# Placing the rows of a Z block on every third partition, in three transfers

## The chip, the cores and the metric

The kernel runs on one core of one Trainium2 chip. The metric is the device time of one execution in microseconds (us). Most quantities below come from one execution that the hardware profiler recorded.

## What is computed

For a batch of 8 sequences of 5696 positions and 128 channels, the reference makes a long convolution by FFT and then a spectral mix:

```python
Xf = np.fft.rfft(x, n=2*S, axis=1)
Hf = np.fft.rfft(h, n=2*S, axis=0)
a = np.fft.irfft(Xf * Hf[None], n=2*S, axis=1)[:, :S, :]      # [8, 5696, 128]
X = np.fft.rfft(a, axis=1)                                      # its first 64 modes are used
Yr = einsum('bmd,mde->bme', Xr, w_r) - einsum('bmd,mde->bme', Xi, w_i)
Yi = einsum('bmd,mde->bme', Xr, w_i) + einsum('bmd,mde->bme', Xi, w_r)
u = a + np.fft.irfft(Y, n=S, axis=1)
out = u + maximum(u @ w_ch, 0)                                  # float32
```

## The kernel before

**The work.** The transform length 2S = 11392 is split as 89 x 128. The kernel does both parts as matrix products in f16: a product over the 45 rows of a sequence that hold data (`a_tile`, `h_tile` and the loop before it), and one over 128 with the matrices `m_sb`. Only 45 of the 89 frequencies of the first part are needed, so a spectrum has 90 rows, 45 real and 45 imaginary parts. The batch is taken as 4 pairs (`g_` from 0 to 3). For each pair, `tick` runs over 23 pairs of frequencies: products on TensorE into `Xs`, multiplication with the spectrum of h on VectorE, the way back over 128 on TensorE into `Zs` (the Z values), a transfer of `Zs` into the DRAM scratch `zscr`, and the products that sum up the 64 modes. After the fourth pair the modes are mixed with the weights `W`.

**The final stage.** `u_tile(i, b)` reads the Z values back in another order. The scratch is cut into 32 blocks, 8 to a pair of sequences. A block is 90 rows (the 45 complex frequencies) of 4096 f16 values, 8 KB a row and 64 KB apart in DRAM, 720 KB in all. `load_zt(i)` fetches block i into one of 15 places: 4 in the tile `Xin` (`x_sb`), 4 in `As`, 7 in `MH`. These tiles held the input, its first transform and the matrices before, so a block waits until its place is free (`after`). Blocks 0 to 3 are issued on GpSimd's queue while the last pair is computed, blocks 4 to 14 on SP when that pair ends, and block i+15 on SP once block i has been used. In `u_tile` a Z block is the stationary operand of 16 products with the matrix `fq_sb`, which carries out the last step of the inverse transform; one product with `ib_sb` adds the inverse of the mixed modes. `Z0` and `Z1` are the first partition of the block and the one behind its last: partitions 19 to 108. The products read partitions 0 to 108, and the matrix has zeros in rows 0 to 18. `o_tile` then multiplies by `w_ch`, applies the maximum on ScalarE (L615), adds on VectorE (L616) into one of 20 `O` tiles, and SP sends it out. An output tile is 256 KB, or 208 or 192 KB at the end of a sequence.

**Order.** A small recorder (`R.add`) lists the instructions of each engine in program order and works out the semaphore waits from named tokens: `reads` and `writes` for data, `after` for other instructions. Each engine issues in that order, so an instruction that waits holds up all behind it on that engine, transfers included. A transfer takes the next semaphore of its ring (`R.rings`); one that takes a semaphore again waits for the transfer that had it.

**The head.** SP issues a few constants, then a row of zeros for the unused half of the last row of each of the two sequences in `x_sb` (tokens `xz`), and then the six pieces of the matrices `m_sb` (tile `MH`), which wait for the first piece of h. After them it issues further constants and filters. GpSimd issues h in three pieces, and then x in six (`x_pieces(0)`), which wait for the second piece of h and for the fourth piece of the matrices. All transfers are recorded by one helper, so they have one line, L283; matrix products are L286, evacuations L276 to L280.

Of the kernel before, what the change touches and what calls it, by code (L numbers as in the profile page):

```python
# [4 lines left out]
P = 128  # L5
# [118 lines left out]
def bass_long_conv_fft__then__afno_spectral_mix_kernel(nc, x, h, moe_w_r, moe_w_i, moe_w_ch, out):  # L124
# [8 lines left out]
    NQ = (NA + 1) // 2  # L133
# [3 lines left out]
    NT = (NQ + 1) // 2  # L137
# [16 lines left out]
    back = 4096.0 / L * np.where(kk == 0, 1.0, 2.0)  # L154
    step = pow(P, -1, NA)
    NW = NA + NQ - 1
    ph = 2.0 * np.pi * ((np.outer(kk, P * np.arange(NW))) % NA) / NA
    fq = np.zeros((P, NW))
    Z0 = 64 - NQ
    Z1 = 64 + NQ  # L160
    fq[Z0:Z1:2] = back[:, None] * np.cos(ph)
    fq[Z0 + 1:Z1:2] = -back[:, None] * np.sin(ph)
    tt = np.arange(N)
    ang = 2.0 * np.pi * np.outer(tt, np.arange(M)) / S
    modes = np.concatenate([np.cos(ang), -np.sin(ang)], axis=1)
# [9 lines left out]
    def const(name, a):  # L175
        return nc.inline_tensor(np.ascontiguousarray(a.astype(np.float16)), name=name)
# [10 lines left out]
    c_z = const("cZ", np.zeros((1, 64 * D)))  # L187
    zs = nc.dram_tensor("zscr", [NP * 2 * NQ * P, 2 * D], F16, kind="Internal")
# [6 lines left out]
    def at(name, cols, dt, off):  # L195
        return nc.alloc_sbuf_tensor_at(name, [P, cols], dt, offset=off)
# [16 lines left out]
    x_sb = at("Xin", P * D, F16, a_x)  # L213
# [23 lines left out]
    NC = 15  # L237
    zt = [(x_sb, P * D, i * 4096) for i in range(4)] + [(a_sb, 2 * AW, i * 4096) for i in range(4)]
# [12 lines left out]
    def ap(t, row, p0, n, off, dims):  # L251
        return bass.AP(t, p0 * row + off, [[row, n]] + [list(d) for d in dims])
# [4 lines left out]
    def pv(bank, off, dims, p0=0, n=P):  # L257
        return bass.AP(ps, p0 * 4096 + bank * 512 + off, [[4096, n]] + [list(d) for d in dims])

    R = Recorder(nc)  # L260
# [3 lines left out]
    def bank(i):  # L264
        return ("bank", i)
# [3 lines left out]
    def evac(dst, src, reads, writes, scale=None, eng=None, after=()):  # L269
        e = eng  # L270
        if e is None:
            turn[0] ^= 1
            e = "scalar" if turn[0] else "vector"
        if e == "scalar":
            if scale is None:
                return R.add(e, lambda h_: h_.copy(dst, src), reads, writes, after=after)  # L276
            return R.add(e, lambda h_: h_.activation(dst, src, COPY, scale=scale), reads, writes, after=after)  # L277
        if scale is None:
            return R.add(e, lambda h_: h_.tensor_copy(dst, src), reads, writes, after=after)  # L279
        return R.add(e, lambda h_: h_.tensor_scalar_mul(dst, src, scale), reads, writes, after=after)  # L280

    def dma(eng, dst, src, ring, reads=(), writes=(), after=()):
        return R.add(eng, lambda h_: h_.dma_start(dst, src), reads, writes, ring=ring, after=after)  # L283

    def mm(o, l, r, st, sp, reads, writes):
        return R.add("tensor", lambda h_: h_.matmul(o, l, r, start=st, stop=sp), reads, writes)  # L286
# [3 lines left out]
    def tile2(slots=3):  # L290
        slot[0] = (slot[0] + 1) % slots
        return 2 * slot[0]
# [4 lines left out]
    half = 64 * D  # L297
    dma("sync", fh_sb[:, :], c_fh.ap(), "c", (), [("fh",)])
    dma("sync", h_in[64 + NQ - 1:64 + NQ, :], c_z.ap(), "c", (), [("hz",)])
    dma("sync", f1_sb[:, :], c_f1.ap(), "c", (), [("f1",)])  # L300
    for b in range(2):
        dma("sync", x_sb[(b + 1) * NQ - 1:(b + 1) * NQ, half:], c_z.ap(), "c", (), [("xz", b)])

    def x_pieces(g_):
        for b in range(2):
            p0, off = b * NQ, x.offset + (2 * g_ + b) * S * D
            for c in range(2):
                yield (x_sb[p0:p0 + NQ - 1, c * half:(c + 1) * half],
                       bass.AP(x.tensor, off + c * half, [[P * D, NQ - 1], [1, half]]), ("xin", b, c))
            yield (x_sb[p0 + NQ - 1:p0 + NQ, 0:TAIL * D],  # L310
                   bass.AP(x.tensor, off + (NQ - 1) * P * D, [[TAIL * D, 1], [1, TAIL * D]]), ("xin", b, 2))

    h_loads = [dma("gpsimd", h_in[64 * c:64 * c + NQ - 1, :],
                   bass.AP(h.tensor, h.offset + c * half, [[P * D, NQ - 1], [1, half]]), "x", (), [("hin", c)])
               for c in range(2)]
# [5 lines left out]
    m_loads = []  # L321
# [2 lines left out]
            m_loads.append(dma("sync", m_sb[i][:, c * CH:(c + 1) * CH], bass.AP(c_m, i * KW + c * CH, [[2 * KW, P], [1, CH]]), "c",  # L324
                (), [("m", i, c)], after=h_loads[:1]))
    for dst, src, tok in x_pieces(0):
        dma("gpsimd", dst, src, "x", (), [tok], after=[h_loads[1], m_loads[3]])
    dma("sync", wi_sb[:, P:2 * P], c_i.ap(), "c", (), [("i16",)])
    dma("sync", fq_sb[:, :], c_fq.ap(), "c", (), [("fq",)])
    dma("sync", wv_sb[:, :], c_w.ap(), "c", (), [("wv",)])  # L330
# [20 lines left out]
    for j in range(16):  # L351
        t = tile2(4)
# [142 lines left out]
    def done_with(toks):  # L495
        return [r for tok in toks for r in R.readers.get(tok, [])[-2:]]

    def load_zt(i):
        g_, c = divmod(i, 8)
        j = i % NC  # L500
        after = []
        if i < 4:
            after = done_with(XT_[:6])
        elif i < NC:
            after = done_with(AST[:1])
            if i >= 8:
                after += done_with([("m", r, c_) for r in range(3) for c_ in range(NCH)] + HST)
        t, row, o = zt[j]
        dma("gpsimd" if i < 4 else "sync", ap(t, row, Z0, 2 * NQ, o, [[1, 4096]]),
            bass.AP(zs, g_ * 2 * NQ * P * 256 + c * 4096, [[P * 256, 2 * NQ], [1, 4096]]),  # L510
            "t" if i < 4 else "u", [("zd", g_, s) for s in range(NT)], [("zt", j)], after=after)

    X_AT = (1, 4, 7, 10, 13, 14)
    W_AT = (16, 18, 20)
# [2 lines left out]
    for g_ in range(NP):  # L517
        more = list(x_pieces(g_ + 1)) if g_ + 1 < NP else []
        todo_a = list(range(32)) if more else []
        for t in range(NT + LM):  # L520
            done = tick(g_, t)
            if t in X_AT and more:
                dst, src, tok = more.pop(0)
                dma("gpsimd", dst, src, "x", (), [tok], after=[done])
            if t in W_AT:
                load_w([done])
            if g_ == NP - 1 and t == NT:
                dma("sync", ib_sb[:, :], c_ib.ap(), "c", (), [("ib",)], after=done_with(AST[:1]))
            if g_ == NP - 1:
                for _ in range(ZT_AT.get(t, 0)):  # L530
                    load_zt(zt_next)
                    zt_next += 1
            if t >= NT:
                for _ in range(4):
                    if todo_a:
                        a_tile(todo_a.pop(0), False)
        modes_out(g_)
        while todo_a:
            a_tile(todo_a.pop(0), True)
        modes_turn(g_)  # L540
# [18 lines left out]
    for b in range(B):  # L559
        bk = 2 + b // 4  # L560
        for half_, yy in ((0, yr), (1, yi)):
            o = ps16[64 * half_:64 * half_ + 64, bk * 1024 + (b % 4) * P:bk * 1024 + (b % 4) * P + P]
# [13 lines left out]
    def u_tile(i, b):  # L576
        g_, c = divmod(i, 8)
        t = tile2(4)
        zt_, row, zo = zt[i % NC]
        for hb in range(2):  # L580
            o = pv(t + hb, 0, [[1, 360]])
            mm(o, c_sb[:, (2 * g_ + b) * P:(2 * g_ + b + 1) * P],
               ib_sb[:, (c * 16 + hb * 8) * NQ:(c * 16 + hb * 8 + 8) * NQ], True, False,
               [("c", g_ // 2), ("ib",)], [bank(t + hb)])
            for pl in range(8):
                o2 = (hb * 8 + pl) * 256 + b * P
                f0 = step * (c * 16 + hb * 8 + pl) % NA
                mm(pv(t + hb, pl * NQ, [[1, NQ]]), ap(zt_, row, 0, Z1, zo + o2, [[1, P]]), fq_sb[0:Z1, f0:f0 + NQ],
                   False, pl == 7, [("zt", i % NC), ("fq",)], [bank(t + hb)])
        ub = i // 2 % 2 * 2 + b  # L590
        n_ev[0] += 1
        evac(bass.AP(u_sb[ub], i % 2 * 16, [[UW, P], [32, NQ], [8, 2], [1, 8]]),
             pv(t, 0, [[1, NQ], [512, 2], [NQ, 8]]), [bank(t), bank(t + 1)],
             [("u", ub, i % 2)], after=g_done, eng="scalar" if n_ev[0] % 8 in (0, 2, 3, 5, 7) else "vector")
# [28 lines left out]
    for v in range(4 * NP):  # L623
        order = [(i, b) for i in (2 * v, 2 * v + 1) for b in range(2)]
        for n, (i, b) in enumerate(order):
            u_tile(i, b)
            for _ in range((2, 1, 2, 1)[n]):
                if todo:
                    o_tile(*todo.pop(0))
            if b and i + NC < 8 * NP:  # L630
                load_zt(i + NC)
        todo = [(v, b, qg) for b in range(2) for qg in range(3)]
# [34 lines left out]
```

## Time and profile before

| What | us |
|---|---|
| median of 3 runs (lowest, highest) | 474.1 (472.33, 479.89) |
| the profiled execution | 469.47 |
| its span, the basis of the profile's times | 467.6 |
| TensorE busy, share of the span | 405.6, 87% |
| VectorE, ScalarE busy | 332.7 and 331.1, 71% each |
| GpSimd busy | 27.6, 6% |
| SP's and ScalarE's hardware queue, share of 16 DMA engines | 57.6% |
| GpSimd's software queue, share of 16 DMA engines | 28.7% |

Times in the profile count from the start of the span. A line such as `45.09 16.84 PE ps L286 x128` of the chain means: at 45.09 us, for 16.84 us, 128 products of L286 on TensorE (PE). SPq and POOLq are the instruction queues of SP and GpSimd; PEld is the load of a stationary operand. The chain is followed back from the last instruction, at each step to what released it. A transfer appears under destination and source: `MH<-cM` are the matrices, `Xin<-zscr`, `As<-zscr` and `MH<-zscr` Z blocks, `out_dram<-O` outputs.

### The profile page before, as it was taken

What the parts mean: (1) busy time and instruction counts of PE and PEld (TensorE: products, weight loads), DVE (VectorE), ACT (ScalarE), POOL (GpSimd) and SP (SyncE); (2) the same over time, 40 slices, a digit from 0 to 9 for tenths busy, and PEclk for the clock granted to TensorE, in tenths of its full rate; (3) what the DMA queues carried; (4) which work ended last, traced back from release to release, by engine and by line L of the source; (5) the groups of instructions that cost most, each with busy time, mean ns of one, the idle gap of its engine ahead of it and who ended that gap; (6) DMA issues with size and microseconds to landing.
All of it is one profiled execution on the core that took longest, in us unless ns stands there. A gap on an engine that the chain in (4) does not pass through costs nothing.

```text
span 467.6 us, 10192 instructions
## 1 busy us (share of the span) xinstructions
PE 405.6 (87%) x4212; PEld 323.4 (69%) x4212; DVE 332.7 (71%) x568; ACT 331.1 (71%) x416; POOL 27.6 (6%) x44
## 2 busy tenths in 40 slices
PE   0589979999979999979999979999689977677993
PEld 0589967776967776976776976775667766466772
DVE  0255879888679988769898679897037766556874
ACT  1235878888878898788888888888038766565773
POOL 1110000010100010100011010000000000000000
PEclk9999999999999999999999999999669999999998
DMA  8995029999919999919999939766999999999998
GB/s 131 315 175 116 1 42 191 260 229 231 195 22 170 265 257 229 197 30 162 254 261 227 176 99 274 208 171 166 305 275 270 319 387 368 354 376 357 326 307 284
DMA packets 96878, 105.04 MB, mean 225 GB/s; under 512 B 22615, under 2 KB 80871, under 8 KB 93031
## 3 DMA queue, kind: packets, MB, share of 16 engines
q1 hardware_dynamic: 78290, 84.11, 57.6%
q0 software_dynamic: 18544, 20.30, 28.7%
q8 instruction: 33, 0.54, 0.5%
q14 instruction: 11, 0.09, 0.0%
HBM read 74.82 MB, written 46.92 MB: 260 GB/s over the span
## 4 chain that ended last, share of the span: by engine, by line
PE 59%; DMA 23%; DVE 8%; ACT 5%; issue 2%; SPq 1%; POOL 1%; DVEq 0%; ACTq 0%; POOLq 0%
PE ps L286 59%; DMA out_dram<-O 13%; DMA Xin<-in_x_dram 5%; DMA Hin<-in_h_dram 2%; DMA MH<-cM 2%; DMA zscr<-Zs 2%; DVE O L616 2%; DVE Pb L441 2%; ACT Xs L277 2%; DVE Xs L446 1%; ACT Zs L276 1%; DVE Xs L479 1%; DVE As L280 1%; DVE UT L279 1%; ACT R L615 1%
## 5 line engine op out<-in xcount | busy, mean ns | idle before, releaser
L277 ACT ACTIVATE Xs<-ps 128x1024 f16<-128x1024 f32 (+1 forms) x92 | 91.3, 1007 | 18.9 <-PE ps L286 18.8
L276 ACT CAST Zs<-ps 128x1024 f16<-128x1024 f32 (+1 forms) x92 | 93.6, 1019 | 13.2 <-PE ps L286 10.8
L286 PE MATMUL ps<-Xs,WV 128*128 128x512 f16 (+1 forms) x368 | 92.9, 375 | 7.5 <-DVE Xs L479 7.3
L286 PE MATMUL ps<-As,MH 128*128 128x256 f16 x720 | 91.7, 273 | 2.5 <-ACT As L277 2.5
L616 DVE TENSOR_TENSOR O<-ps,R 128x512 f32<-128x512 f32 (+2 forms) x96 | 62.6, 686 | 34.8 <-DMA out_dram<-O 13.3
L441 DVE TENSOR_TENSOR Pb<-Xs,MH 128x1024 f16<-128x1024 f16 (+1 forms) x92 | 62.4, 679 | 23.6 <-ACT Xs L277 23.4
L286 PEld LDWEIGHTS ps<-As,MH 128*128 128x128 f16 x720 | 70.1, 98 | 12.1 <-DVE As L280 2.0
L479 DVE TENSOR_TENSOR Xs<-Xs,Pb 128x512 f16<-128x512 f16 (+1 forms) x184 | 77.5, 424 | 0.1
L286 PE MATMUL ps<-F,Xin 90*128 90x256 f16 x512 | 72.0, 296 | 1.4 <-ACT Zs L276 0.4
L286 PEld LDWEIGHTS ps<-F,Xin 90*128 90x128 f16 x512 | 68.4, 226 | 4.2 <-ACT Zs L276 1.1
L280 DVE TENSOR_SCALAR As<-ps 128x720 f16<-128x720 f32 x59 | 56.2, 953 | 20.7 <-PE ps L286 18.5
L615 ACT ACTIVATE R<-ps 128x512 f32<-128x512 f32 (+2 forms) x96 | 53.9, 600 | 20.4 <-PE ps L286 20.3
L277 ACT ACTIVATE As<-ps 128x720 f16<-128x720 f32 x69 | 57.2, 840 | 13.2 <-PE ps L286 12.4
L446 DVE TENSOR_TENSOR Xs<-Xs,MH 128x1024 f16<-128x1024 f16 (+1 forms) x92 | 61.9, 673 | 0.1
L286 PEld LDWEIGHTS ps<-Xs,WV 128*128 128x128 f16 x368 | 34.9, 98 | 33.3 <-DVE Xs L479 10.4
L286 PE MATMUL ps<-IBs,C 128*128 128x360 f16 x128 | 42.2, 330 | 17.5 <-DVE O L616 17.1
L286 PE MATMUL ps<-WI,UT 128*128 128x256 f16 (+2 forms) x384 | 55.8, 280 | 0.4
L286 PE MATMUL ps<-Zs,Gs 128*128 128x256 f16 x360 | 54.3, 273 | 0.7 <-ACT Zs L276 0.7
L286 PEld LDWEIGHTS ps<-Zs,Gs 128*128 128x128 f16 x360 | 34.8, 98 | 23.8 <-ACT Zs L276 3.1
L276 ACT CAST UT<-ps 128x720 f16<-128x720 f32 x40 | 30.3, 758 | 19.7 <-PE ps L286 18.2
L286 PEld LDWEIGHTS ps<-WI,UT 128*128 128x128 f16 (+2 forms) x384 | 40.3, 134 | 3.0 <-DVE UT L279 1.3
L286 PEld LDWEIGHTS ps<-IBs,C 128*128 128x128 f16 x128 | 12.5, 98 | 26.4 <-DVE O L616 24.8
(45 smaller groups left out, 263.4 us busy)
## 6 DMA issues: line engine op xcount, KB each, us to landing
zscr<-Zs SPq DMA_DIRECT2D x88, 256.0 KB, 5.6
out_dram<-O SPq DMA_DIRECT2D x64, 256.0 KB, 12.4
Gs<-cG SPq DMA_DIRECT2D x88, 128.0 KB, 5.8
Xin<-in_x_dram POOLq DMA_DIRECT2D x16, 704.0 KB, 8.3
MH<-zscr SPq DMA_DIRECT2D x14, 720.0 KB, 17.6
As<-zscr SPq DMA_DIRECT2D x8, 720.0 KB, 13.9
Xin<-zscr SPq DMA_DIRECT2D x6, 720.0 KB, 19.7
out_dram<-O SPq DMA_DIRECT2D x16, 208.0 KB
```

The lines of the kernel that those rows point to most:

```text
L276: return R.add(e, lambda h_: h_.copy(dst, src), reads, writes, after=after)
L277: return R.add(e, lambda h_: h_.activation(dst, src, COPY, scale=scale), reads, writes, after=after)
L279: return R.add(e, lambda h_: h_.tensor_copy(dst, src), reads, writes, after=after)
L280: return R.add(e, lambda h_: h_.tensor_scalar_mul(dst, src, scale), reads, writes, after=after)
L286: return R.add("tensor", lambda h_: h_.matmul(o, l, r, start=st, stop=sp), reads, writes)
L441: R.add("vector", lambda e: e.tensor_tensor(pbv, xv, hv[1], MULT), [tx] + HST, [tp], after=[h_done])
L446: R.add("vector", lambda e: e.tensor_tensor(xv, xv, hv[0], MULT), [tx] + HST, [tx])
L479: R.add("vector", lambda e: e.tensor_tensor(a, a, b, ADD if part else SUB), [("xs", s % NX), ("pb", s % NB_)], [("xs", s % NX), ("y", s % ...
L615: R.add("scalar", lambda e: e.activation(rv, src_r, RELU), bk, [("r", i % NR)], after=[mixed])
L616: R.add("vector", lambda e: e.tensor_tensor(ov, src_u, rv, ADD), bk + [("r", i % NR)], [("o", i % NO)], after=[mixed] if i % NO < 16 - NR ...
```

## The change

A block's 90 rows go to other partitions, in three transfers instead of one: rows 0 to 41 to partitions 0, 3, ... 123, rows 42 to 83 to partitions 1, 4, ... 124, and rows 84 to 89 to partitions 2, 23, 44, 65, 86, 107. The matrix `fq` has its rows in the same places and zeros between, and the products read partitions 0 to 124. The three transfers of a block share one semaphore: the second and third go back to the same place in the ring and drop its wait. A product waits for all three.

Since the products now read rows of `x_sb` above 89 that nothing had written, VectorE fills partitions 64 to 127 of `x_sb` with zeros at the start. The second zero row (`xz`, b = 1, which lies in partition 89) and the transfers of x wait for that fill.

```diff
-    Z0 = 64 - NQ
-    Z1 = 64 + NQ
-    fq[Z0:Z1:2] = back[:, None] * np.cos(ph)
-    fq[Z0 + 1:Z1:2] = -back[:, None] * np.sin(ph)
+    ZROWS = ((0, 42, 0, 3), (42, 42, 1, 3), (84, 6, 2, 21))
+    fz = np.stack([back[:, None] * np.cos(ph), -back[:, None] * np.sin(ph)], axis=1).reshape(2 * NQ, NW)
+    for r0, n, p0, st in ZROWS:
+        fq[p0:p0 + n * st:st] = fz[r0:r0 + n]
+    Z1 = 125
...
+    x_zero = R.add("vector", lambda e: e.memset(x_sb[64:, :], 0.0), [], [("x0",)])
     for b in range(2):
-        dma("sync", x_sb[(b + 1) * NQ - 1:(b + 1) * NQ, half:], c_z.ap(), "c", (), [("xz", b)])
+        dma("sync", x_sb[(b + 1) * NQ - 1:(b + 1) * NQ, half:], c_z.ap(), "c", (), [("xz", b)],
+            after=[x_zero] if b else [])
...
     for dst, src, tok in x_pieces(0):
-        dma("gpsimd", dst, src, "x", (), [tok], after=[h_loads[1], m_loads[3]])
+        dma("gpsimd", dst, src, "x", (), [tok], after=[h_loads[1], m_loads[3], x_zero])
...
-        dma("gpsimd" if i < 4 else "sync", ap(t, row, Z0, 2 * NQ, o, [[1, 4096]]),
-            bass.AP(zs, g_ * 2 * NQ * P * 256 + c * 4096, [[P * 256, 2 * NQ], [1, 4096]]),
-            "t" if i < 4 else "u", [("zd", g_, s) for s in range(NT)], [("zt", j)], after=after)
+        name = "t" if i < 4 else "u"
+        ring = R.rings[name]
+        place = ring[-1]
+        for l, (r0, n, p0, st) in enumerate(ZROWS):
+            if l:
+                ring[-1], ring[place][2] = place, None
+            dma("gpsimd" if i < 4 else "sync", bass.AP(t, p0 * row + o, [[st * row, n], [1, 4096]]),
+                bass.AP(zs, (g_ * 2 * NQ + r0) * P * 256 + c * 4096, [[P * 256, n], [1, 4096]]),
+                name, [("zd", g_, s) for s in range(NT)], [("zt", j, l)], after=after)
...
-                   False, pl == 7, [("zt", i % NC), ("fq",)], [bank(t + hb)])
+                   False, pl == 7, [("zt", i % NC, l) for l in range(3)] + [("fq",)], [bank(t + hb)])
```

## The prediction

> **What bounds the kernel now.** I read four views in this order: the slices of the span, the chain that ended last in order of time, the stretches of the final stage, and the groups by shape. All are of one execution, whose own time was 469.47 us with a span of 467.6; the median of the runs is 474.1. I work out differences against the execution and add them to the median; the 4.6 us between the two is no more than the runs differ among themselves (472.33 to 479.89), and about 2% (9.5 us) is what a measurement of this kernel can tell from no change.
>
> ```profile
> PEclk9999999999999999999999999999669999999998
> DMA  8995029999919999919999939766999999999998
> GB/s 131 315 175 116 1 42 191 260 229 231 195 22 170 265 257 229 197 30 162 254 261 227 176 99 274 208 171 166 305 275 270 319 387 368 354 376 357 326 307 284
> ```
> A slice is 11.7 us. Two regions have full DMA engines: the first three slices, where the inputs come in, and everything from slice 28 (327 us) on. Slices 28 to 30, in which almost only Z blocks are read back, reach some 270 to 305 GB/s at the same busy share at which slices 32 and 35 reach 375 to 387. Both regions are on the chain:
>
> ```profile
> 1.24 9.19 DMA Hin<-in_h_dram
> 10.45 0.35 SPq L283
> ...
> 11.78 9.11 DMA MH<-cM
> 20.89 0.28 issue
> 21.17 2.51 POOL Xin L283 x5
> 23.68 21.32 DMA Xin<-in_x_dram
> 45.00 0.09 issue
> 45.09 16.84 PE ps L286 x128
> ...
> 362.95 15.31 DMA out_dram<-O
> ...
> 418.44 13.74 DMA out_dram<-O
> ```
> At the head, everything hangs on: h lands, SP issues the matrices, the fourth lands (20.89), x is issued, x lands (45.00), TensorE starts. Between 45 and 327 the chain is TensorE with short evacuations. At the end it is output transfers that take 13 to 15 us to land, because they queue behind Z blocks; the 20 output tiles are all taken, and VectorE waits for one.
>
> ```profile
> 342.00:363.00 21.00, 20.29 (x309) 15.99 (x309) 13.38 (x20) 13.62 (x23) 0.00 (x0) 0.87 0.96 272
> 378.00:400.00 22.00, 16.00 (x254) 13.00 (x253) 13.47 (x20) 13.57 (x24) 0.00 (x0) 1.00 1.00 375
> 400.00:420.00 20.00, 14.49 (x230) 12.10 (x229) 11.67 (x18) 11.81 (x20) 0.00 (x0) 1.00 0.99 363
> ```
> The columns are the stretch, its length, busy time of TensorE, weight load, VectorE, ScalarE and GpSimd, granted clock, DMA share, GB/s. At 272 GB/s a Z block (90 rows of 8 KB, 737,280 B) takes 2.71 us. So DMA time in the final stage moves the end, until about 445, where outputs land 3 to 6 us after issue and the engines' own pace takes over.
>
> **The change: the fill at the head.** VectorE gets a fill of 64 x 16384 f16 elements at the very start. SP's second zero row (issued at 2.2 us) now waits for it, and SP issues in order.
>
> ```profile
> 1.91 0.57 SPq L283 DMA_DIRECT2D Xin<-cZ  x2
> 10.45 2.72 SPq L283 DMA_DIRECT2D MH<-cM  x6
> ...
> L280 DVE TENSOR_SCALAR Ah<-ps 128x720 f16<-128x720 f32 x8 | 7.3, 907 | 24.8 <-PE ps L286 24.8
> L280 DVE TENSOR_SCALAR MH<-ps 128x1024 f16<-128x1024 f32 x5 | 6.1, 1225 | 5.1 <-PE ps L286 5.1
> L365 DVE TENSOR_SCALAR MH<-MH 128x1920 f16<-128x1920 f16 x3 | 1.8, 652 | 0.0
> ```
> No fill by VectorE is in the trace. The cheap end is L365, packed f16 from SBUF: 652/1920 = 0.34 ns an element, 5.6 us. The dear end is L280 with its fixed part: 907/720 = 1.26 ns, 20.6 us. Between the two forms of L280, (1225-907)/304 = 1.05 ns an element: 17.2 us. I take 17.2: the fill has no packed f16 source, which is what sets the fast row apart. Beginning near 0.75 us (ScalarE's first instruction is at 0.73) it ends at 18.0.
>
> [...]
>
> SP now reaches the matrices at 18.3 us (the zero row's issue takes 0.29) instead of 10.45. The delay is not passed on in full: in the trace the first matrix transfers stood behind h, which landed at 16.4 to 16.6, and then landed 1.2 us apart (17.3, 18.5, 19.7, 20.9). Issued at 18.3 into empty queues, with 1.4 us to the first data (F's first part came 1.5 us after its issue) and four times 1.2, the fourth lands near 24.6 to 25.0: 4.0 us late. x is issued 4 us later and needs its 23.8 us again (the same matrices, constants and filters stand beside it), so it lands at 49.0. TensorE ends the transform of h at 44.7 and now idles 4.3 us. **Head, on the chain: +4.0.** The transform of h hides 0.3 us of it, no more. After 327.1, when TensorE had only 8-column products, the granted clock fell to 0.5 at 330.4; a 4.3 us idle stretch may do the same here. At half clock a tile of four 256-column products would take some 0.85 us instead of 0.53 (16.84/32); for some 7 us (how long the clock stayed low after dense work began at 340.1) that is 2.8. Between 0 and 2.8 I take 1.5. So the head gives +5.5; its bounds are 0 (a fill under 9.7 us is over before h lands at 10.43, when SP would be free anyway) and +10 (20.6 us: 3.4 more, with the clock).
>
> **The Z blocks.** 28 of 32 blocks go out from SP. By the trace's semaphore records, a transfer of 13 groups of rows shows 14 updates, one of 12 shows 13, a single row 2, while 128 rows show 16: one per DMA engine used, plus one at once if fewer than 16. A 90-row block shows 16, the first 0.5 to 0.8 us after issue and the rest 8 to 27 us later: 15 engines with 6 rows each. By the same pattern (the largest divisor up to 16) 42 rows go over 14 engines, 3 each, and 6 rows over 6. I assume all three start from the same engine. Then six engines carry 3+3+1 = 7 rows of each block, instead of 6, and outputs need all engines, so those six set the pace.
>
> [...]
>
> What a row costs decides. In the packet records an 8 KB row takes 0.309 us at the quickest; in 342 to 363 the mean is 0.459 (the rate gives 2.71/6 = 0.45), with all 15 engines stretched alike, and in 378 to 420, beside outputs, 0.345 to 0.36. Matrix rows over 128 partitions move 3840 B in 0.154 us, unstretched, and x rows, also 64 KB apart in memory, are mostly unstretched too (1.227 us for 32 KB read). So the stretch may come from where the Z rows land, which the change alters. Bounds for the new row: 0.309 and 0.452 in the Z-only stretch, 0.309 and 0.35 beside outputs. I take 0.36, the row of the mixed stretch, and 0.325.
> - 13 blocks land between 336 and 370, nearly alone: 7 x 0.36 = 2.52 against 2.71, -0.19 each, -2.5 (bounds 2.16, -7.2; 3.16, +5.9).
> - 15 blocks land between 373 and 432 beside outputs: 7 x 0.325 = 2.28 against 6 x 0.35 = 2.10, +0.18 each, +2.6 (bounds +0.9, +5.3).
>
> **Queue: +0.1**, from -6.3 to +11.2.
>
> The rest: SP issues 56 more transfers at 0.3 to 0.5 us. A round of two blocks and six outputs is then twelve issues, 4 x 0.6 + 2 x 0.83 + 6 x 0.45 = 6.8 us, under the 8.1 that a round takes in the mixed stretch (two between the outputs issued at 380.55 and 396.70); SP waited 44.8 us for VectorE's results there. Cost 0; at no cover it would be 1.4 a round. GpSimd issues 8 more at 0.53, between 274 and 281, with nothing behind them. The Z products load 125 rows instead of 109: 96 ns at 109 rows and 98 at 128, so 0.
>
> **Sum:** 5.5 + 0.1 = +5.6, that is 474.1 + 5.6 = 479.7, say 480 (the execution would be 475).
>
> **The rivals.**
> - *Spread rows move freely.* Rows at 0.309 in both stretches: -6.3, and with the head +5.5, 473. For it: the unstretched matrix rows. Against: six engines drift behind the others by a row per block, so what is spread at the first row mixes later. With a short fill too it is 468. [...]
> - *The fill is short.* Over before 10.4: head 0, time 474. For it: VectorE's fast row. Against: it has no source to pack.
> - *Seven rows and no relief* (slower). If the stretch comes from reading rows 64 KB apart, unchanged, rows stay at 0.452 and 0.35 and the sixth share becomes a seventh: +11.2, with the head +16.7, 491. It decides from a row over 2.71/7 = 0.387 us in the Z-only stretch. For it: all engines were stretched alike and at once, as by one common limit. Against: the x rows. [...]
> - *Nothing happens*, with both terms within 1 us: 474, folded into the short fill.
>
> **Chances.** The forecast 0.45, free rows 0.2 (a third of it with a short fill), short fill 0.13, no relief 0.22. Faster by over 2% (under 464.6) needs the lowest end of both terms and luck: 0.07. Slower by over 2% (over 483.6): no relief, and the dear third of the forecast where the clock drops and the queue loses 2: 0.32. Within: 0.61. Range 467 to 490: from free rows with a short fill to just under no relief.
>
> **What would show it.** A fill on VectorE from 0.7 to 18 us; SP's matrix issues at 18.3; x landing at 49, TensorE starting there; the granted clock just after. Blocks with 15, 15 and 7 updates; the stretch after the modes at 2.5 us a block; the sixteen engines finishing an output unevenly. The prediction falls if the fill ends before 10.4, if Z rows in the first stretch stay at 0.45 or go to 0.31, or if the three parts of a block start on different engines, which would even out the seventh row.

## The result and the profile after

| | before | after |
|---|---|---|
| median of 22 runs each, us (lowest, highest) | 474.04 (467.72, 489.15) | 477.86 (475.14, 487.9) |
| ratio after to before, with 95% interval | | 1.012 [1.0095, 1.0144] |
| the profiled execution, us (its span) | 469.47 (467.6) | 480.17 (478.4) |
| from the first u tile to the end, us | 127.5 | 136.6 |
| everything ahead of it, us | 340.2 | 341.8 |

The change costs 1.2%, about 5.7 us. Some executions of either kernel were disturbed and run longer; the ratios, here and below, leave them out, while the medians count all. The two profiled executions lie 10.7 us apart, since that of before is near the fast end of its runs and that of after near the slow end; the differences between them show where the time went, not how much it is.

The slices of the span after the change (one is now 12.0 us):

```profile
DMA  7994039999749999739999378667989999999998
GB/s 128 328 164 102 1 52 201 260 233 232 144 60 197 266 239 228 133 64 237 232 241 213 90 240 232 176 170 251 256 246 262 351 355 341 318 330 341 307 308 257
```

The region from slice 28 on is longer and slower: it reached 354 to 387 GB/s before at its height, now 318 to 355. The stretches of the final stage, with the columns of the prediction:

```profile
342.00:363.00 21.00, 19.75 (x291) 15.41 (x290) 11.92 (x18) 12.78 (x22) 0.00 (x0) 0.82 0.90 246
378.00:400.00 22.00, 16.57 (x247) 13.43 (x244) 13.02 (x19) 12.38 (x21) 0.00 (x0) 0.95 0.94 350
400.00:420.00 20.00, 14.03 (x221) 11.51 (x219) 11.35 (x18) 12.29 (x21) 0.00 (x0) 1.00 0.92 329
```

The rate is lower by 7 to 10% (246 for 272, 350 for 375, 329 for 363 GB/s), and so is the share of time in which the DMA engines are busy: 0.90 to 0.94 for 0.96 to 1.00. They are not so much slower while they work as idle more often.

The head, by engine (VectorE, SP's queue, GpSimd; start, length, instruction):

```profile
2.51 6.88 DVE L303 MEMSET Xin<- 64x8192 uint32 x1 [2.51 <-issue]
...
1.92 7.74 SPq L285 DMA_DIRECT2D Xin<-cZ  x2
11.43 2.78 SPq L285 DMA_DIRECT2D MH<-cM  x6
...
21.30 3.01 POOL L285 DMA_DIRECT2D Xin<-in_x_dram  x6 [18.37 <-DMA MH<-cM]
```

The fill begins at 2.51 us and is over at 9.39, before h's first piece lands (11.42; 10.43 before). SP stands at its second zero row for most of 7.74 us, but it would have waited for h in any case. The fourth matrix lands at 21.02 (20.89 before), x is issued at 21.30 (21.17) and lands at 45.65 (45.00). TensorE starts on x 0.65 us later than before.

Near the end the chain now holds longer runs of SP's own issues. Before, they were one Z transfer and the end of an output's issue, about 0.8 us at a time (from 379.70 and from 395.78); now they are:

```profile
400.95 0.56 SPq L285
401.56 0.85 SPq L285
402.41 0.05 issue
402.46 0.82 SPq L285
403.32 0.75 SPq L285
404.11 0.65 SPq L285
404.81 10.50 DMA out_dram<-O
```

402.46 to 404.76 are the three transfers of one Z block, and the output behind them on SP's queue goes out at 404.81. The granted clock of TensorE is no rival: from 365 to 425 us it was 0.97 after the change, and 0.91 in experiment 1, which lost nothing.

### The profile page after: what moved, and what is told of

It is laid out like the page before. It is cut to its first block, busy times and chain, and to the rows that moved or that the text cites. A ratio compares the mean times of both kernels' runs of the same rounds, so it can differ in the third digit from the quotient of the medians.

```text
span 478.4 us, 10257 instructions
## 1 busy us (share of the span) xinstructions
PE 409.8 (86%) x4212; PEld 326.1 (68%) x4212; DVE 339.5 (71%) x569; ACT 331.1 (69%) x416; POOL 31.2 (7%) x52
## 4 chain that ended last, share of the span: by engine, by line
PE 60%; DMA 21%; DVE 8%; ACT 5%; issue 2%; SPq 2%; POOL 0%; DVEq 0%; ACTq 0%; POOLq 0%
PE ps L288 59%; DMA out_dram<-O 12%; DMA zscr<-Zs 6%; DMA Hin<-in_h_dram 3%; DVE O L626 2%; SPq L285 2%; ACT Zs L278 2%; DVE Pb L445 1%; ACT Xs L279 1%; DVE Xs L450 1%; DVE Xs L483 1%; DVE UT L281 1%; DVE As L282 1%; ACT R L625 1%; ACT As L279 1%
## 5 line engine op out<-in xcount | busy, mean ns | idle before, releaser
L288 PE MATMUL ps<-IBs,C 128*128 128x360 f16 x128 | 43.4, 339 | 24.6 <-DVE O L626 24.1
L288 PE MATMUL ps<-WI,UT 128*128 128x256 f16 (+2 forms) x384 | 57.3, 285 | 0.4
L288 PEld LDWEIGHTS ps<-IBs,C 128*128 128x128 f16 x128 | 12.7, 99 | 33.2 <-DVE O L626 31.3
```

## The experiments

A ratio is to the kernel before on the same chip. "Rows" are the mean times of the 8 KB packets of Z blocks in the trace, of one execution each.

**1. The fill alone.** The kernel before, with the fill and the two waits for it.

```diff
+    x_zero = R.add("vector", lambda e: e.memset(x_sb[64:, :], 0.0), [], [("x0",)])
...
+            after=[x_zero] if b else [])
...
-        dma("gpsimd", dst, src, "x", (), [tok], after=[h_loads[1], m_loads[3]])
+        dma("gpsimd", dst, src, "x", (), [tok], after=[h_loads[1], m_loads[3], x_zero])
```

> The kernel before with the fill and its two waits alone; Z blocks as before. In the profile of the changed kernel the fill took 6.88 us (2.51 to 9.39) and SP issued the matrices at 11.43 instead of 10.45, x landed at 45.6 instead of 45.0. Theory 'the head costs nothing': ratio to the kernel before 0.998 to 1.003, and TensorE's first product on x within 1 us of 45.1. Rival 'the head is the loss': 1.008 or more, about +4 us. The fill should again stand as 64x8192 words of about 6.9 us.

Ratio 0.9959 [0.9921, 0.9997]: the head costs nothing, and the whole loss lies in the Z blocks. This kernel does more than the one before and came out 0.4% faster, so a difference of that size is not to be read as an effect. Its rows, untouched by the edit, took 0.470 us in 342 to 363.

**2. Three transfers of 42, 42 and 6 rows in the old places**, without the fill.

```diff
+    ZROWS = ((0, 42, 19, 1), (42, 42, 61, 1), (84, 6, 103, 1))
...
+        for l, (r0, n, p0, st) in enumerate(ZROWS):
```

> The kernel before, its Z block on partitions 19 to 108 as before, but in three transfers of 42, 42 and 6 rows; no fill. Theory 'seventh row' (six DMA engines carry 7 rows of a block, the others 6) and theory 'issues' (three transfers at 0.65 to 0.75 us on SP) both expect the changed kernel's ratio, 1.008 to 1.016, and a Z-only stretch at 0.46 us a row. Theory 'places' (where the rows land sets the row time) expects a ratio unlike the changed kernel's: above 1.02 if the new places help, about 1.00 if they hurt.

Ratio 1.021 [1.0162, 1.0258]. Splitting into these parts costs more than the whole change, so for these parts the new places give about 0.9% back.

**3. The same with 45, 30 and 15 rows**, which by the pattern of the update counts (16 for a block of 90 rows before; 15, 15 and 7 after) fifteen engines share evenly, 6 rows each.

```diff
+    ZROWS = ((0, 45, 19, 1), (45, 30, 64, 1), (75, 15, 94, 1))
```

> As the run before it, but in three transfers of 45, 30 and 15 rows: each over 15 engines, 3+2+1 = 6 rows on each, no seventh row. Theory 'seventh row': 0.998 to 1.004. Theory 'issues': 1.008 to 1.016, SP's waits for VectorE's results shrinking from 44.8 us to about 23 as in the changed kernel. A block should show 16+16+16 updates.

Ratio 1.018 [1.0124, 1.0235]: no seventh row, and no better, and more than either theory expected. Rows took 0.548 us in 342 to 363, 0.555 in 363 to 378 and 0.424 in 378 to 400, where the single transfer of before has 0.459, 0.388 and 0.345. So with the pieces side by side the rows were longer; experiment 5 shows how far that can be taken for the cause.

**4. Two spread transfers**: the kernel after, with 45 rows on every second partition, twice (products read 126 partitions).

```diff
-    ZROWS = ((0, 42, 0, 3), (42, 42, 1, 3), (84, 6, 2, 21))
+    ZROWS = ((0, 45, 0, 2), (45, 45, 37, 2))
```

> The changed kernel with two transfers of 45 rows a block, on every second partition from 0 and from 37 (to 88 and 125): 3+3 rows on each of 15 engines, fill and waits as in the changed kernel. Theory 'seventh row': 0.998 to 1.004. Theory 'issues': half of the loss, about 1.006. Theory 'places': row times in the Z-only stretch leave 0.46 us, below 0.40 if spread rows help. If neither seventh row nor issues matter but spreading hurts, 1.010 or more.

Ratio 0.9952 [0.9916, 0.9988], the same as with the fill alone. Two transfers instead of three, by the same pattern 6 rows on each of fifteen engines, and the loss is gone. Rows are 0.487 us in 342 to 363 and 0.383 in 378 to 400, no shorter than those of the single transfer.

**5. The source 68 KB apart**, in the kernel before.

```diff
+    ZP = P * 256 + 2048
+    zs = nc.dram_tensor("zscr", [NP * 2 * NQ, ZP], F16, kind="Internal")
```

> The kernel before with the rows of the DRAM scratch 68 KB apart instead of 64 KB; partitions and transfers as before. Theory 'the stretch comes from reading rows 64 KB apart': the mean row in the Z-only stretch (342 to 363 us) falls from 0.46 us towards 0.31, the ratio to 0.985 or less. Theory 'the stretch comes from where rows land': the row stays at 0.44 to 0.48 us, ratio 0.996 to 1.004.

Ratio 1.0004 [0.9963, 1.0045]; rows no shorter but longer, 0.517 us in 342 to 363 and 0.509 in 363 to 378, which neither theory had. The 64 KB between source rows isn't what stretches them; one other distance was tried. Up to 378 us these rows are nearly as long as those of experiment 3 (from there to 400, 0.354 against 0.424), and no time was lost. The length of a row in one execution is therefore no measure of a loss, and that longer rows are what slowed experiments 2, 3 and 8 is not shown.

**6. All blocks of the changed kernel on GpSimd's queue.**

```diff
-            dma("gpsimd" if i < 4 else "sync", bass.AP(t, p0 * row + o, [[st * row, n], [1, 4096]]),
+            dma("gpsimd", bass.AP(t, p0 * row + o, [[st * row, n], [1, 4096]]),
```

> The changed kernel with all 32 blocks issued on GpSimd's queue instead of 28 on SP. In the profile of the changed kernel SP spends 0.65 to 0.8 us on each third of a block and issues the first output at 358.4 us, 7 us after its tile was ready. Theory 'SP's issues': the loss goes, ratio 0.99 to 1.003, first output issued near 352. Theory 'DMA work alone' (seventh row, row times): ratio stays at 1.008 to 1.016. GpSimd's transfers have a queue of their own, so outputs no longer stand behind blocks in one queue; a ratio below 0.99 would have to be put down to that.

Ratio 1.0195 [1.0143, 1.0247], which says nothing of either theory: the blocks overtook the transfer of `ib_sb`, which had stood ahead of them on SP's queue. It landed at 355.7 us instead of 333.9, and the u tiles began at 355.8 instead of 341.8. From there to the end it took 125.8 us, against 136.6, but with blocks that had a start of 14 us. Experiments 10 to 12 avoid this.

**7. Three even spread transfers**: the kernel after, 30 rows each on every fourth partition, by the same pattern 6 rows per engine.

```diff
-    ZROWS = ((0, 42, 0, 3), (42, 42, 1, 3), (84, 6, 2, 21))
+    ZROWS = ((0, 30, 0, 4), (30, 30, 1, 4), (60, 30, 2, 4))
```

> The changed kernel with its three transfers of 30 rows each, on every fourth partition from 0, 1 and 2: 2+2+2 rows on each of 15 engines, no seventh row, three issues of spread rows on SP as in the changed kernel. Theory 'seventh row': ratio 0.996 to 1.004. Theory 'SP's issues': 1.008 to 1.014, like the changed kernel, with SP spending 0.7 us on each.

Ratio 1.0206 [1.0159, 1.0254], more than expected, although rows are now 0.392 us in 342 to 363 (beside outputs, in 378 to 420, 0.41). SP's queue in the trace (start, length, and what it issued; x3 are three transfers):

```profile
361.00 3.12 SPq L285 DMA_DIRECT2D out_dram<-O  x3
364.17 2.49 SPq L285 DMA_DIRECT2D Xin<-zscr  x3
...
384.46 2.97 SPq L285 DMA_DIRECT2D As<-zscr  x3
387.47 2.10 SPq L285 DMA_DIRECT2D out_dram<-O  x3
```

Three issues for a block take 2.5 to 3 us; the first output tile was ready at 350.7 and went out at 361.0. Outputs land 4 to 5 us after their issue, so nothing waits behind the DMA engines; but a tile lies 28.6 us between its last write and its issue (tiles 31 to 50). Most of the 20 tiles wait in front of SP. Against experiment 4, the row count per engine is the same, and the third issue and the places (every fourth partition for every second) differ: 2.5%. In experiment 4 a block and three outputs take SP less: 1.66 us from 394.32 on for the block, 2.12 from 396.03 on for the outputs, and the next block follows at 398.20.

The seventh row is gone here, and yet the loss is larger than with it. Against experiment 3, even parts in the old places (1.018), the spread places gain nothing.

**8. Two transfers in the old places**, 45 and 45 rows side by side.

```diff
+    ZROWS = ((0, 45, 19, 1), (45, 45, 64, 1))
```

> The kernel before with two transfers of 45 rows on partitions 19 to 63 and 64 to 108, 3+3 rows on each of 15 engines; beside the run with two transfers on every second partition (0.995) only the places differ. Theory 'places': ratio 1.010 to 1.018, rows in the Z-only stretch at 0.52 to 0.56 us, as in the three transfers in place. Theory 'number of transfers' (places don't matter): ratio 0.993 to 1.000, rows at 0.46 to 0.49 us.

Ratio 1.0116 [1.0059, 1.0173] against 0.9952 of experiment 4. Split in two, the spread places are worth some 1.6%; the fill, which only experiment 4 has, costs nothing.

**9. SP's time by itself**: the kernel before, with two transfers of 42 rows of 4 bytes to spread partitions behind each of the blocks 4 to 31. They carry 336 bytes a block.

```diff
+        for l in range(2 if i >= 4 else 0):
+            dma("sync", bass.AP(dm_sb, l * 64 + i * 2, [[3 * 128, 42], [1, 2]]),
+                bass.AP(c_i, 0, [[P, 42], [1, 2]]), "d", (), [("dm", i, l)])
```

> The kernel before with two extra transfers on SP behind each of blocks 4 to 31, each of 42 spread rows but only 4 bytes a row: SP's issue time of the changed kernel (0.7 to 0.8 us each, some 2.0 us a block instead of 0.5) with next to no bytes, no seventh row and the old places. Theory 'SP's issues': first output issued near 355 us instead of 349.7, a round of two blocks and six outputs at 8.2 us of SP alone, ratio 1.004 to 1.012. Theory 'DMA work alone': 0.997 to 1.003.

Ratio 1.0098 [1.0063, 1.0133]. The Z blocks are those of before, in one transfer each. What is added is some 1.5 us of SP per block, as the change adds 1.7, and 84 tiny packets a block, which with those of their semaphores took some 2 us of each DMA engine over all blocks. Four fifths of the change's loss come with it; how much of that the packets have was not separated.

**10. Experiment 7 on GpSimd's queue**, where the blocks 4 to 14 wait for `ib_sb`.

```diff
-            after = done_with(AST[:1])
+            after = done_with(AST[:1]) + ib_load
...
-            dma("gpsimd" if i < 4 else "sync", bass.AP(t, p0 * row + o, [[st * row, n], [1, 4096]]),
+            dma("gpsimd", bass.AP(t, p0 * row + o, [[st * row, n], [1, 4096]]),
```

> Three spread transfers of 30 rows (as in the run with ratio 1.021, whose outputs landed 4.6 us after issue, so that DMA was not what they waited for), but all blocks on GpSimd, and blocks 4 to 14 waiting for the matrix of the inverse modes, which the earlier run with blocks on GpSimd had made late by 14 us. Theory 'SP's issues bound that run': ratio 0.980 to 0.995. Theory 'DMA work bounds it': 1.01 or more.

Ratio 0.9891 [0.985, 0.9933], median 469.01 against 473.34: this is 1.1% faster than the kernel before. From the u tiles to the end it takes 126.8 us.

**11. The single transfer of before on GpSimd's queue**, in the old places, with the same wait.

```diff
-        dma("gpsimd" if i < 4 else "sync", ap(t, row, Z0, 2 * NQ, o, [[1, 4096]]),
+        dma("gpsimd", ap(t, row, Z0, 2 * NQ, o, [[1, 4096]]),
```

> The kernel before with its one transfer per block, old places, all blocks on GpSimd, blocks 4 to 14 waiting for the matrix of the inverse modes. It tells what the queue alone does, beside the run with three spread transfers on GpSimd: 0.990 to 1.005 if the places and not the queue make the gain; as fast as that run or faster if the queue makes it.

Ratio 1.0209 [1.0138, 1.028], from two executions only, and slower than was expected of the queue or of the places alone (0.990 to 1.005). The queue by itself is no gain. Experiment 10 has more transfers and other places as well, and which of the two it needs was not separated.

**12. The changed kernel's 42, 42 and 6 rows on GpSimd's queue**, the edit of 10 without that of 7.

> The changed kernel's own 42, 42 and 6 rows, all blocks on GpSimd, blocks 4 to 14 waiting for the matrix of the inverse modes; beside the run with three times 30 rows on GpSimd (0.989) only the rows per transfer and their places differ, and SP's issues are out of both. Theory 'seventh row': slower than that run by 0.5% or more, ratio 0.994 to 1.005, and outputs whose 16 parts land far apart, as in the changed kernel (a quarter within 4 us, the last after 12). Theory 'SP's issues were all of the loss': 0.985 to 0.993, like that run.

Ratio 1.0133 [1.0084, 1.0181], more than the expected 0.994 to 1.005. Against experiment 10, with neither kernel's Z issues on SP, the uneven parts and their places cost 2.4%. The stretch from 365 to 425 us in experiment 10,

```profile
365.00:425.00 60.00, 49.88 (x640) 36.85 (x640) 33.75 (x50) 34.20 (x58) 13.30 (x27) 0.77 0.98 379
```

and in experiment 12:

```profile
365.00:425.00 60.00, 42.44 (x475) 29.40 (x474) 25.29 (x37) 25.42 (x42) 13.69 (x27) 0.66 0.91 330
```

379 against 330 GB/s, at 0.98 and 0.91 of the engines busy. The granted clock is lower too (0.66 for 0.77); whether that follows from the slower stage or adds to it isn't shown. Rows hardly differ (0.32 and 0.33 us in 378 to 420). What differs in the semaphore records is how an output lands. The semaphore of an output tile of 256 KB takes 16 updates, which I read as one for each engine's part as it lands; here are the 16 times from issue to update, in us, of one output issued some 403 to 415 us into each kernel:

```
before         3.83 7.95 8.89 10.11 10.15 10.19 10.45 12.11 12.33 12.82 | 13.12 13.38 13.96 14.25 14.88 15.15
after          2.58 2.62 3.19  3.28  3.29  3.30  3.35  3.36  3.60  3.70 |  8.24  8.69  9.20  9.54  9.98 10.50
experiment 7   2.82 2.96 3.04  3.10  3.11  3.13  3.25  3.26  3.47  3.55 |  3.62  3.68  3.75  3.76  4.53  4.84
experiment 10  2.54 3.99 4.64  7.96  9.48  9.83 10.60 11.44 11.72 11.93 | 12.24 12.30 12.53 12.76 12.81 13.20
experiment 12  4.17 4.40 4.42  4.43  4.48  4.55  4.58  4.59  4.63  4.65 | 12.64 12.79 13.35 13.76 14.02 14.12
```

After and in experiment 12, ten parts land close together (2.58 to 3.70 us, and 4.17 to 4.65), and six land 4 to 10 us later. Where the rows divide evenly there are no such two groups; experiment 2, with 42, 42 and 6 rows in the old places, has them too (at 413.5 us ten parts by 4.85 us and six from 8.83 to 14.34). On GpSimd's queue a block of three transfers shows 48 updates, 16 each, so there the counts don't tell which engines had a row, and the two groups are the only sign of how the rows lay.

## Why the prediction was right, and where it wasn't

The forecast of 480 us lies 2 us from the median, and its +5.6 us on the 5.7 of the ratio. That is luck. The sum is right, its terms aren't: +5.5 of it was to come from the head, and that came to nothing, while terms put at 0.1 and 0 made the loss. Two of the signs by which the prediction said it would fall came: the fill was over before 10.4, and Z rows in the first stretch stayed at 0.45 or more.

- **The fill: wrong.** I took 17.2 us between 5.6 and 20.6, from VectorE's evacuations, and kept "the fill is short" as a rival with a chance of 0.13. It took 6.88 us, near the cheap end, and the rival's rule (over before 10.4, head 0) holds to the letter; experiment 1 has the same fill and no loss. My argument, that the fill has no packed f16 source, was read from L365 and L280 alone, which differ in more than that. The profile has the fill as 64x8192 uint32, half as many elements as I counted, 0.84 ns each, so 0.42 ns per f16 element beside the 1.05 I took and L365's 0.34. The price of a delay in the granted clock after an idle TensorE fell with it: the granted clock was 1.00 from 39 to 332 us.
- **The division over the engines: right.** A block shows 37 updates in the records, 15, 15 and 7. That the three parts start from the same engine was an assumption; the two groups of ten and six are what it implies on SP's queue. No view numbers the engines, so that the six are those with seven rows is read from the groups alone.
- **What a row costs: wrong, on the side of the rival "seven rows and no relief".** I took 0.36 and 0.325 us. Measured after the change: 0.474 in 342 to 363, and 0.342 to 0.367 in 378 to 420, as long as before (0.459, or 0.470 in experiment 1, and 0.345 to 0.362). The deciding point, 0.387 us in the first stretch, is passed. By the prediction's own lines that makes a seventh row at 0.355 in 15 blocks, +5.3, beside outputs instead of +2.6, and a loss in place of the gain in the first stretch (246 GB/s, 3.00 us a block for 2.71, so +3.8 for 13). Together that is 9.1, more than the 5.7 measured, so this sum isn't the account either. And the reason I gave that rival fell too: rows 64 KB apart in the source are not the cause (experiment 5), and where rows land does matter for the time (experiments 4 and 8), only that every third partition brought no shorter rows on SP's queue.
- **SP's issues at no cost: wrong.** I had 0.45 us an issue and a round of 6.8 us under 8.1. A spread issue takes more than a contiguous one: 0.73 to 0.82 us for 42 rows and 0.65 even for 6, against 0.40 for 45 or 30 adjacent rows in experiment 3 when nothing held them up (0.52 for the first one behind an output). Half a round, one block and three outputs, is then 4.5 us of issuing, 9.0 a round, and SP has hardly a pause:

```profile
395.81 2.10 SPq L285 DMA_DIRECT2D out_dram<-O  x3
397.95 2.29 SPq L285 DMA_DIRECT2D MH<-zscr  x3
400.27 2.14 SPq L285 DMA_DIRECT2D out_dram<-O  x3
402.46 2.30 SPq L285 DMA_DIRECT2D MH<-zscr  x3
```

That is after; the same queue before:

```profile
396.11 0.54 SPq L283 DMA_DIRECT2D MH<-zscr  x1
396.70 3.48 SPq L283 DMA_DIRECT2D out_dram<-O  x3
400.23 0.53 SPq L283 DMA_DIRECT2D MH<-zscr  x1
```

  From 374.7 to 416.5 us half a round takes 4.64 us on average, of which 4.5 are issues; before it was 4.13 (372.4 to 417.8). The six engines are not what holds it there: the last part of an output landed 12.7 us after its issue at 377 and 9.9 at 414, so their queues were emptying. The first output tile, ready at 351.3, went out at 358.4, behind 24 Z transfers. The runs with spread rows on SP, and experiment 9, fall in order by this term: at its quickest half a round takes SP 3.9 us in experiment 4, 4.4 in experiment 9, 4.5 after the change and 4.7 in experiment 7, and the ratios are 0.995, 1.010, 1.012 and 1.021. Only experiment 4 is under the 4.13 that half a round takes before the change. Experiments 2, 3 and 8 do not fit this order: their adjacent issues are cheap, and yet they lose 1.2 to 2.1%. What holds them is open.
- **The cover that I named was none.** SP's 44.8 us "for VectorE's results" was read as idle time. But before the change a tile lay 13.6 us between its last write and its issue (tiles 31 to 50), so VectorE had long been done when SP stood at the first output behind each block for 1.4 to 2.1 us. What held it there the profile doesn't name, and no run tested it. After the change those waits are gone and issues stand in their place, and the tile lies 18.3 us.
- **Right at no cost:** GpSimd's issues (twelve in 6.06 us from 275.93 on, where four had taken 2.09), and the products over 125 rows (a load of a Z block took 96 to 102 ns on average by tile, before and after); ahead of the final stage only 1.6 us are lost in all.

So either limit alone makes a kernel slower: SP's issue time without a seventh row (experiment 7, 2.1%; experiment 9, 1.0%), and the uneven parts, with their places, without SP's issue time (experiment 12, 1.3%). In the changed kernel both are there, and taking the seventh row away on SP's queue didn't help (experiment 7). How its 1.2% divides isn't settled by these runs; that SP is the nearer limit from 375 to 416 us is read from its 4.64 us for half a round, 4.5 of them issues.

Splitting a block cost 1.2 to 2.1% in experiments 2, 3, 7 and 8, all on SP's queue. It cost nothing in experiment 4, where the kernel with two transfers a block took no longer than before (0.995), and in experiment 10 three transfers a block beat one by 1.1%.

## What to carry to other kernels

Take the price of an extra transfer from a row with the same kind of destination (here an issue took 0.73 to 0.82 us for 42 spread rows and 0.40 for 45 or 30 adjacent ones), and add up a whole round of the queue that issues it: a wait that the profile puts down to a producer is only spare time if the producer really finished last. Split a transfer so that the rows divide evenly over the engines of all parts together: here, where they did not, six of an output's 16 parts landed 4 to 10 us behind the other ten. Three spread transfers beat the single one here only when both held, with even parts issued on a queue that had time (0.989).

## What the runs showed of the hardware

- With nothing holding it up, an issue to spread partitions cost SP 0.65 us for 6 rows and 0.73 to 0.80 for 30 to 45 (up to 0.85 behind an output); to adjacent ones it cost 0.30 for 6, 0.32 to 0.41 for 15 to 45, and 0.32 to 0.46 for 90 (0.53 behind an output). Spread rows of 4 bytes were no cheaper than rows of 8 KB (0.72 to 0.77). Why, no view shows.
- An 8 KB row into SBUF took 0.307 us at the quickest. On average, in 342 to 363 us on SP's queue, it took 0.459, 0.470 and 0.517 for 90 adjacent partitions in one transfer (before, experiments 1 and 5), 0.548 for three adjacent pieces, 0.487 on every second, 0.474 on every third and 0.392 on every fourth partition. On GpSimd's queue it was 0.393 on every third and 0.388 on every fourth. What sets it, the runs don't show.
- Where 42, 42 and 6 rows made a block, six of the 16 parts of an output landed 4 to 10 us behind the other ten, on GpSimd's queue (experiment 12) as on SP's. The same three spread, even transfers that lost 2.1% on SP's queue won 1.1% on GpSimd's.
